# A gated scan and a top-1 mixture of experts on one core: new numbers for the planner that orders the instructions

## The chip, the core and the metric

The kernel runs on one core of a Trainium2 chip. The metric is the device time of one execution in microseconds (us). The kernel before took 938.03, 938.60 and 939.13 us in three runs; the median is 938.6 us. A profile was taken of one further execution, and all rows below come from it.

## The reference

Four sequences of 5056 steps and 256 channels run through a gated scan. The 20224 results then go, one expert each, through a two-layer network with 8 experts and 1024 hidden units.

```python
a_t     = exp(8 * sigmoid(r_gate) * log(sigmoid(a_param)))
x_gated = sqrt(max(1 - a_t * a_t, 1e-6)) * sigmoid(i_gate) * x
h       = a_t[:, t] * h + x_gated[:, t]           # over the 5056 steps
logits  = y @ w_gate + modality_bias[modality_id]
e_idx   = argmax(logits);  gate_w = softmax(logits)[e_idx]
out     = gate_w * (relu(y @ w1[e_idx]) @ w2[e_idx])
```

## The kernel before

**Chunks.** The steps are cut into 22 chunks (`STEPS`): one of 96 steps, three of 128, seventeen of 256, one of 224. A chunk's three inputs `a`, `g` and `x` (the recurrence gate, the input gate, the data) are loaded through SP's queue (L592). ScalarE (ACT) takes tanh of `g` (L636) and of `a` (L654), an exp (L660), a square and a square root (L665, L669). VectorE (DVE) takes the largest value of `x` (L840), combines the inputs (L642, L674) and runs the scan (L691). The scan's result is split into a high and a low half-precision part (ACT L888, DVE L900), which replace the input in the tile `a`.

**Routing.** TensorE (PE) computes the logits (`psl`, L913), DVE turns them into a destination index for each token (`di`, L1040), SP transposes the split result into rows (`rt<-a`, L941), and GpSimd (POOL) scatters the rows into a table in DRAM sorted by expert (`rows<-rt,di`, L1141), 128 tokens each time. Chunk 0 takes 3 such scatters, chunks 1 to 3 take 4, the chunks of 256 steps take 8. POOL also copies and adds the modality bias (`mf`, `mg`, `bm`, `bn`, L799 to L825).

**Pages.** The two experts that most tokens chose are called hot; their weights are loaded first (`wr0` to `wr3`: first and second layer of the one, then of the other), scaled and split into high and low parts (`hw0_0`, `hw0_1`, `hw1_0`, `hw1_1`; some low parts on PE and ACT as `pl`, L458, L459 and L461, others on DVE). A page is a group of rows of one expert. The first two pages of 128 rows come straight from a pick on PE (`Xfirst`). Then come twenty pages of 256 rows, from about 230 us pages of 512, and at the end four small ones. For a page SP reads the rows back transposed (`X<-rows`, L1404) with their token numbers (`mt`, L1405). PE computes the first layer into `ph` (L1502), ACT and DVE make `H` of it (L1430, L1432), PE computes the second layer into `po` (L1548), ACT scales it (`ot`, L1449), and POOL scatters it to the output (L1460). Names with a number are pages: `ph2_0` is the first quarter of the first layer of page 2, `X2` its rows. A page can't be read before the scatters that filled it have landed.

**Order.** Nothing is reordered on the chip: each engine runs its list in the order in which the program was built. A planner in Python makes that order. Each piece of work is a generator that yields an engine, an estimated duration and a condition; `run` takes the earliest startable piece, within a small window the one with the lowest rank, and emits it. The ranks are `BASE[kind] + C_STEP * chunk + RANK[kind][chunk]` (function `place`); the weights have ranks of their own (`W_RANK`, `W_LOW`). Loads have estimated landing times, which stand in `mark["load", c, name]`; work on a chunk is planned from that time. `HI` says whether ACT or DVE makes the high part of a weight, `START` the order of the first loads (a digit is a chunk, `w` a weight), `TURN` is a price on changing ACT's function table, `ON_DVE` the chunk from which small pieces move from DVE to POOL.

**Fills.** Where the plan sees PE idle for over 0.5 us (`FILL_MIN`), `fill` puts matmuls on constants there (L339, tile `fill`), 1.25 times as many as the planned gap would hold. They compute nothing that is used; they stand in PE's list like other work.

```python
n = (at - t) * FILL / 0.214 if t > COLD else (at - t) / 0.427
```

Of the kernel before, what the change touches and what calls it, by code (L numbers as in the profile page):

```python
# [18 lines left out]
B, S, D, E, FF = 4, 5056, 256, 8, 1024  # L19
# [28 lines left out]
PART = 8  # L48
BACKLOG = 6500
LOOK = 384  # L50
HI = ["A", "AD", "D", "DA", "A", "D"]
LO = "PPPDDD"
START = "0 1 w w w w 2"
MODALITY = 11.81
MODALITY_LAST = 17.39
TURN = 0.0
HALVED = 9
PACED = 2
AHEAD = 9.62
AHEAD_OF_ROWS = 2.88  # L60
LAND = 1.19
SHOW = 0.46
W_AT = 9.0
C_STEP = 3.08
GROW = 1.01
SIZE_LAG = 2.99
SIZE_LATE = 6.0
LATE = 9
LAG_LATE = 5.0
SLACK = 5.0  # L70
SLACK_EARLY = 0.0
EARLY = 7
ON_DVE = 8
BIAS_RANK = -2.93
URGENT = 0.0
ROW_STEP = 2.0
LAG = 3.0
W_RANK = [24.2, 31.2, -6.7, 1.6]
W_LOW = [6.7, 7.3, -8.0, 8.8]
PICK_AT = 8.34  # L80
PICK = 11.62


RANK = {
    "load": [0.0, 0.0, 3.0, 1.1, 0.0, 1.8, -0.6, 0.0, 0.0, 7.7],
    "scan": [0.0, 0.0, 1.5, 6.8, 1.3, -0.1, -3.1, 3.3, 0.5],
    "gate": [-2.7, -1.5, -6.0, 0.0, 0.6, -1.5, 0.0, 0.0, 0.0, -6.1],
    "size": [0.0, 0.0, 0.0, 0.0, 0.0, 0.0, 2.1, 0.0, 9.5, 4.6],
    "split": [-5.2, 0.9, 0.0, -0.5, 0.5, -2.0, 1.3, -1.3, 0.0, -1.6],
    "low": [0.0, 1.6, -3.0, -1.2, 0.0, 0.0, 5.4, 0.3, -5.6, 0.3],  # L90
    "route": [-1.2, 0.0, -3.2, -3.1, 0.0, 0.0, -4.1, 0.0, -3.7],
    "gates": [0.0, 0.0, 2.9, -2.1, 0.0, 0.0, -2.0, 0.0, -5.9],
    "rows": [-2.5, -3.4, 0.0, -9.8, 0.8, 0.0, -3.4, 2.1, -1.7],
}
BASE = {
    "load": 10, "scan": 11, "gate": 11.1, "size": 11.05, "split": 10, "low": 10, "route": 9, "gates": 9.5, "rows": 10,
# [32 lines left out]
def kernel(  # L129
# [24 lines left out]
    rows = dram.tile([NULLS + BIG, ROW], I32, name="rows")  # L154
# [24 lines left out]
    low = mb1  # L179
# [105 lines left out]
    mark = {"ch": 5.0}  # L285
# [4 lines left out]
    plan = {"end": 0.0}  # L290
# [54 lines left out]
    def run():  # L345
        while threads:
# [13 lines left out]
            turns = lambda th: eng == "ACT" and len(th.req) > 4 and th.req[4] != table[0]  # L360
            th = min(near, key=lambda th: (th.prio[eng != "PE"] + TURN * turns(th), th.start))
            dur = th.req[1]
# [69 lines left out]
    def convert(k, name, raw, to, sc, prio, urgent, then):  # L432
# [32 lines left out]
        for v in range(2):  # L465
            vs = slice(FF * v, FF * v + FF)
            src, hi = raw[:, vs], to[:, vs]
            if HI[k][v % len(HI[k])] == "A":
                yield "ACT", 1.0, None
# [8 lines left out]
    loads, seq = [], 0  # L478
    for what in START.split():
        if what == "w":  # L480
# [90 lines left out]
    def load_chunk(c):  # L571

        t0, T = CHUNKS[c]
        cols = 2 * B * T
        base = 2 * B * t0
        z = T / 256
        got = tiles[c] = []
        if f"{c}" in loads:
            yield "SP", 0.0, seen(("turn", loads.index(f"{c}") - 1)), 0.0
        else:  # L580
            yield "SP", 0.0, allof(drained(sum(B * t for _, t in CHUNKS[: c + 1]) - BACKLOG), seen(("load", c - 1))), -3.0
        n = max(1, T // P)
        for name, src in (("a", rs), ("g", gs), ("x", xs)):
            tag = "H" if c == 0 and name != "g" else name
            for i in range(n):
                yield "DMA", 2.9 * z / n, allof(room(tag) if i == 0 else seen(), paced(c)), -9.0
                if i == 0:
                    tickets[c, name] = tag, take(tag)
                    t = (pm if tag == "H" else pa).tile([P, cols], F32, name=f"{name}{c}", tag=tag, bufs=BUFS[tag])
                    got.append(t)  # L590
                w = cols // n
                ins = LOADS.dma_start(t[:, i * w : (i + 1) * w], src[:, base + i * w : base + (i + 1) * w])  # L592
                if c >= PACED:
                    tc.add_manual_dep(
                        ins.ins, pace[-2], mybir.DependencyInfo(mybir.DependencyClass.Sync, mybir.DependencyReason.DATA)
                    )
                pace.append(ins.ins.name)
                landed.append(plan["end"] + 0.1)
            mark["load", c, name] = plan["end"] + (SLACK if c >= LATE else SLACK_EARLY if c > 1 else 0.0)
        if c == 0:  # L600
            yield "DMA", 0.2, None, -9.0
            nc.sync.dma_start(wg, w_gate.rearrange("(h p) e -> p h e", p=P))
            yield "DMA", 0.2, None, -9.0
            nc.sync.dma_start(mb, mbias.rearrange("m e -> (m e)").partition_broadcast(P))
            yield "DMA", 0.5, None, -9.0
            nc.sync.dma_start(mid, modality.bitcast(I32).rearrange("p (c two) -> p c two", two=2))
        went(f"{c}")
        mark["load", c] = plan["end"]
        if c + 1 < NC:
            start_chunk(c + 1)  # L610
# [143 lines left out]
    def modality_order():  # L754
# [18 lines left out]
        while c < NC:  # L773
            n = 1
            while c + n < NC and CHUNKS[c + n][1] == CHUNKS[c][1]:
                n += 1
            add(modality_part(c, n, mq, left, tx), (0, 9 if c == 0 else min(place("load", c), MODALITY_LAST) - 0.5), plan["end"])
            c += n
# [144 lines left out]
    def rows_part(c, j):  # L923
# [759 lines left out]
```

## Time and profile before

| quantity | value |
|---|---|
| median of three runs | 938.6 us |
| the profiled execution's own time | 936.79 us |
| span of its profile | 935.1 us |
| mean granted TensorE clock | 0.996 |
| DVE, ACT, POOL busy, share of the span | 69%, 63%, 52% |
| HBM read, written | 70.86 MB, 44.48 MB |

The span runs from the first to the last instruction; 1.69 us of the execution's own time lie around it. An engine's share is its busy time over the span. Averages hide the stages here: the scan's work on DVE and ACT ends well before PE's, so a stage has to be read by a window of its own. In rows of a timeline, a bracket gives the idle time of the engine just before the row and what ended it.

### The profile page before, as it was taken

The page shows a single profiled execution, that of the slowest core. Times are in us where ns is not written, and L with a number is a line of the kernel's source. Part 1 is how long each engine was busy: PE and PEld are TensorE (multiplying, and loading weights), DVE is VectorE, ACT ScalarE, POOL GpSimd, SP SyncE. Part 2 cuts the span into 40 slices and gives each one's busy share as a digit, 9 for nine tenths or more (in the row PEclk, how much of TensorE's full clock was granted, in tenths as well). Part 3 has the DMA queues.
Part 4 walks back from the last instruction along what each step waited for, and adds up shares of the span by engine and source line. Part 5 has one row for each costly group of instructions (what it writes and reads, how often), then busy time and mean ns, then how long its engine had stood idle before and what let it go on. Part 6 is the DMA issues. An engine that isn't in the chain of part 4 may idle for free. (4 is left out here: it accounts for less than half of the span.)

```text
span 935.1 us, 19529 instructions
## 1 busy us (share of the span) xinstructions
PE 918.8 (98%) x7195; PEld 656.8 (70%) x7195; DVE 645.2 (69%) x1493; ACT 591.0 (63%) x865; POOL 487.8 (52%) x683
## 2 busy tenths in 40 slices
PE   8989899999999999999999999999999999999997
PEld 4567788888887676666666666666666666666796
DVE  7979899988788878788378767878763234423521
ACT  8978769678767777576667558577643335333422
POOL 6545467556463576466646546645664535422222
PEclk9999999999999999999999999999999999999999
DMA  8878998898969696866993985884562435213110
GB/s 312 197 211 202 244 241 247 179 284 185 229 124 225 219 197 152 254 125 160 222 214 108 251 200 159 213 229 128 117 123 72 108 104 163 80 46 125 41 43 25
DMA packets 226940, 157.90 MB, mean 169 GB/s; under 512 B 195665, under 2 KB 200146, under 8 KB 226834
## 3 DMA queue, kind: packets, MB, share of 16 engines
q1 hardware_dynamic: 210562, 112.57, 52.9%
q0 software_dynamic: 16128, 43.98, 13.7%
q8 instruction: 58, 0.95, 0.4%
q14 instruction: 48, 0.39, 0.1%
q10 hardware_dynamic: 144, 0.00, 0.0%
HBM read 70.86 MB, written 44.48 MB: 123 GB/s over the span
## 5 line engine op out<-in xcount | busy, mean ns | idle before, releaser
L1502 PE MATMUL ph<-X,hw 128*128 128x512 f16 (+1 forms) x2400 | 452.6, 333 | 6.1 <-DMA X<-rows 6.1
L1502 PEld LDWEIGHTS <-hw 128*128 128x128 f16 x2496 | 237.9, 98 | 137.3 <-DMA X<-rows 7.8
L1548 PE MATMUL po<-hw,H 128*128 128x256 f16 x2448 | 298.5, 273 | 0.1
L1460 POOL DMA_INDIRECT out_dram<-ot,mt x160 | 183.7, 1148 | 216.3 <-ACT ot L1449 167.2
L1548 PEld LDWEIGHTS <-H 128*128 128x128 f16 x2496 | 241.3, 98 | 51.1 <-issue 0.8
L1141 POOL DMA_INDIRECT rows<-rt,di x158 | 181.2, 1147 | 168.0 <-PE ph L1502 77.7
L1432 DVE SCALAR_TENSOR_TENSOR H<-ph,H 128x512 f16<-128x512 f32 (+1 forms) x216 | 143.7, 668 | 155.9 <-ACT H L1430 154.6
L1430 ACT ACTIVATE H<-ph 128x512 f16<-128x512 f32 (+1 forms) x216 | 124.0, 577 | 133.7 <-PE ph L1502 128.8
L1548 PE MATMUL po<-hw,Hb 128*128 128x256 f16 x1344 | 165.1, 273 | 0.0
L1548 PEld LDWEIGHTS <-Hb 128*128 128x128 f16 x1344 | 131.0, 98 | 36.3 <-issue 0.4
L1432 DVE SCALAR_TENSOR_TENSOR Hb<-ph,Hb 128x512 f16<-128x512 f32 x112 | 76.9, 687 | 91.4 <-ACT Hb L1430 90.7
L1449 ACT ACTIVATE ot<-po,gt 128x256 f32<-128x256 f32 x160 | 75.5, 472 | 91.4 <-PE po L1548 75.1
L1430 ACT ACTIVATE Hb<-ph 128x512 f16<-128x512 f32 x112 | 66.6, 595 | 104.7 <-PE ph L1502 102.0
L691 DVE TENSOR_TENSOR_SCAN g<-a,g 128x512 f32<-128x512 f32 (+2 forms) x77 | 94.0, 1241 | 0.6
L900 DVE SCALAR_TENSOR_TENSOR a<-g,scy,a 128x512 f16<-128x512 f32 (+3 forms) x88 | 58.2, 693 | 4.5 <-ACT a L888 4.2
L888 ACT ACTIVATE a<-g,scy 128x512 f16<-128x512 f32 (+3 forms) x88 | 55.5, 669 | 1.5 <-DVE g L691 1.5
L660 ACT ACTIVATE a<-a,ch 128x1024 f32<-128x1024 f32 (+3 forms) x44 | 49.5, 1148 | 0.0
L840 DVE TENSOR_REDUCE top<-x 128x2 f32<-128x1024 f32 (+4 forms) x35 | 46.6, 1345 | 4.2 <-DMA x<-in_x_dram 4.2
L674 DVE SCALAR_TENSOR_TENSOR g<-x,g 128x1024 f32<-128x1024 f32 (+2 forms) x39 | 47.5, 1231 | 2.1 <-ACT x L669 2.1
L642 DVE SCALAR_TENSOR_TENSOR g<-g,x 128x1024 f32<-128x1024 f32 (+2 forms) x39 | 47.6, 1232 | 0.0
L669 ACT ACTIVATE x<-x,quarter 128x1024 f32<-128x1024 f32 (+3 forms) x35 | 43.8, 1255 | 0.3
L654 ACT ACTIVATE a<-a 128x1024 f32<-128x1024 f32 (+3 forms) x35 | 40.6, 1162 | 3.4 <-DMA a<-in_r_gate_dram 3.1
(220 smaller groups left out, 666.4 us busy)
## 6 DMA issues: line engine op xcount, KB each, us to landing
a<-in_r_gate_dram SPq DMA_DIRECT2D x37, 512.0 KB
g<-in_i_gate_dram SPq DMA_DIRECT2D x37, 512.0 KB
x<-in_x_dram SPq DMA_DIRECT2D x37, 512.0 KB
wr<-in_moe_w_dram SPq DMA_DIRECT2D x4, 1024.0 KB
cw<-in_moe_w_dram SPq DMA_DIRECT2D x4, 1024.0 KB
out_dram<-ot,mt POOLq DMA_INDIRECT x160
rows<-rt,di POOLq DMA_INDIRECT x158
rt<-a SPq DMA_TRANSPOSE x88
```

What stands on the lines that cost most here:

```text
L642: nc.vector.scalar_tensor_tensor(out=g, in0=g, scalar=1.0, in1=x, op0=ALU.add, op1=ALU.mult)
L660: nc.scalar.activation(sl, sl, AF.Exp, scale=ch[:, h : h + 1], bias=ch[:, h : h + 1])
L691: nc.vector.tensor_tensor_scan(out=gi, data0=ai, data1=gi, initial=0.0, op0=ALU.mult, op1=ALU.add)
L888: nc.scalar.activation(ys[:, 0, :, g], yg[:, :, g, :].rearrange("p h (k b) -> p h k b", b=Q), AF.Copy, scale=sc[:, g : g + 1])
L900: nc.vector.scalar_tensor_tensor(out=ys[:, 1, :, g], in0=yg[:, :, g, :].rearrange("p h (k b) -> p h k b", b=Q), scalar=sc[:, g : g + 1], i ...
L1141: ins = nc.gpsimd.indirect_dma_start(out=rows[:, :], out_offset=bass.IndirectOffsetOnAxis(ap=idx, axis=0), in_=src, in_offset=None, bounds ...
L1430: nc.scalar.activation(hi, src, AF.Relu)
L1432: nc.vector.scalar_tensor_tensor(out=lo, in0=src, scalar=0.0, in1=hi, op0=ALU.max, op1=ALU.subtract)
L1449: nc.scalar.activation(t.ot[a // 2][:, a % 2, :], po, AF.Copy, scale=t.gt[:, a : a + 1])
L1460: ins = nc.gpsimd.indirect_dma_start(out=out[:, :], out_offset=bass.IndirectOffsetOnAxis(ap=t.mt[:, a, 0:1], axis=0), in_=t.ot[a // 2][:, ...
L1502: ins = nc.tensor.matmul(to, wv[:, s, k, f * P : (f + 1) * P], cur.X[:, 2 * x + k, :], start=(m == 0), stop=(m == len(mm) - 1))
L1548: ins = nc.tensor.matmul(po, H[:, hx, fi, a * P : (a + 1) * P], wv[:, wx, f], start=(f == 0 and m == 0), stop=(f == NF - 1 and m == 2))
```

## The change

Constants and rank tables of the planner get other numbers, and one line changes: a chunk's inputs were planned to be there at their estimated landing for chunks 2 to 8; now the `x` input of these chunks (the third to the ninth) is taken to land 1.2 us later. The table of ranks (`RANK`, some 80 numbers) is replaced as a whole; one row of it stands for all.

```diff
-HI = ["A", "AD", "D", "DA", "A", "D"]
+HI = ["AD", "AD", "D", "AD", "A", "D"]
-START = "0 1 w w w w 2"
-MODALITY = 11.81
-MODALITY_LAST = 17.39
-TURN = 0.0
+START = "0 w 1 w w w 2"
+MODALITY = 13.01
+MODALITY_LAST = 12.02
+TURN = 0.68
...
-AHEAD = 9.62
-AHEAD_OF_ROWS = 2.88
-LAND = 1.19
-SHOW = 0.46
-W_AT = 9.0
-C_STEP = 3.08
+AHEAD = 7.78
+AHEAD_OF_ROWS = 1.82
+LAND = 1.22
+SHOW = 0.58
+W_AT = 8
+C_STEP = 3.31
...
-SIZE_LAG = 2.99
+SIZE_LAG = 5.95
...
-SLACK_EARLY = 0.0
-EARLY = 7
-ON_DVE = 8
-BIAS_RANK = -2.93
+MARGIN = {(c, 'x'): 1.2 for c in range(2, 9)}
+EARLY = 9
+ON_DVE = 7
+BIAS_RANK = -1.39
...
-W_RANK = [24.2, 31.2, -6.7, 1.6]
-W_LOW = [6.7, 7.3, -8.0, 8.8]
-PICK_AT = 8.34
-PICK = 11.62
+W_RANK = [15.4, 22.1, -1.8, 3.8]
+W_LOW = [14.7, 8.3, -17.0, 8.6]
+PICK_AT = 8.49
+PICK = 12.87
...
-    "load": [0.0, 0.0, 3.0, 1.1, 0.0, 1.8, -0.6, 0.0, 0.0, 7.7],
+    "load": [0.0, -6.1, 0.0, 1.0, 2.9, -1.2, 1.6, -2.3, 0.0, 0.1],
...
-            mark["load", c, name] = plan["end"] + (SLACK if c >= LATE else SLACK_EARLY if c > 1 else 0.0)
+            mark["load", c, name] = plan["end"] + (SLACK if c >= LATE else MARGIN.get((c, name), 0.0))
```

What is computed stays the same, and so do the counts of the page matmuls: 3840 of the second layer (L1548) and, of the first (L1502), 192 with 128 columns, 1056 with 256 and 1344 with 512, in the same pages and in the same sizes. The fills change: 143 before, 139 now. Their places move too. Before, 70 stand ahead of `ph0_0`, the first page matmul, none from there to `po0_0`, 20 between `po0_0` and `ph2_0`, and 53 behind `ph2_0`. Now 69 stand ahead of `ph0_0`, 55 between `ph1_0` and `po0_0`, 5 between `po0_0` and `ph2_0`, and 10 behind `ph2_0`. All of them stand ahead of `ph16_0` in both. Of the second layer of page 1, 24 matmuls (`po1_0` in four groups of six) stood ahead of `ph2_0` before and stand behind it now.

Three places show how the lists move.

**TensorE, around the last two low parts of the first hot expert's second layer.** `pl1_2` and `pl1_3` are these low parts, `nid` a constant, `psl1` the counts of chunk 1. Before, both stand ahead of the first page:

```order
L458 MATMUL pl1_2_891<-wr1_285,dg1_786 128x512
L459 LDWEIGHTS nid_153
L459 MATMUL pl1_2_891<-hw0_1_229,nid_153 128x512
L458 MATMUL pl1_3_902<-wr1_285,dg1_786 128x512
L459 LDWEIGHTS nid_153
L459 MATMUL pl1_3_902<-hw0_1_229,nid_153 128x512
L1013 LDWEIGHTS um1_157
L1013 MATMUL psl1_806<-oh1_908,um1_157 128x32
```

Now they stand between fills, behind `ph0` and the first quarter of `ph1`:

```order
L339 LDWEIGHTS onesb_81
L339 MATMUL fill31_1088<-onesb_81 128x512
L458 MATMUL pl1_2_1092<-wr1_292,dg1_612 128x512
L459 LDWEIGHTS nid_153
L459 MATMUL pl1_2_1092<-hw0_1_229,nid_153 128x512
L458 MATMUL pl1_3_1102<-wr1_292,dg1_612 128x512
L459 LDWEIGHTS nid_153
L459 MATMUL pl1_3_1102<-hw0_1_229,nid_153 128x512
L339 LDWEIGHTS onesb_81
L339 MATMUL fill34_1126<-onesb_81 128x512
```

The two low parts moved behind the first page's first layer, and with them the earliest place at which `po0_0`, the first matmul of a second layer, can stand.

**ScalarE, around the inputs of chunk 4.** `a4` and `g4` are that chunk's gates, `a2` the split of chunk 2, `hw0_1` the second-layer weights of the first hot expert. Before:

```order
L654 ACTIVATE a4_928<-a4_928 128x2048
L1430 ACTIVATE H1_1020<-ph1_2_1089 128x256
L1430 ACTIVATE H1_1020<-ph1_3_1114 128x256
L660 ACTIVATE a4_928<-a4_928,ch_89 128x1024 x2
L888 ACTIVATE a2_404<-g2_453,scy2_867 128x8x32 x2
L1449 ACTIVATE ot1_0_1140<-po1_0_1141,gt1_1148 128x256
L888 ACTIVATE a2_404<-g2_453,scy2_867 128x8x32 x2
L636 ACTIVATE g4_1016<-g4_1016 128x2048
```

Now:

```order
L654 ACT_TABLE_LOAD
L654 ACTIVATE a4_952<-a4_952 128x2048
L665 ACTIVATE x3_827<-a3_746 128x1024
L636 ACTIVATE g4_1001<-g4_1001 128x2048
L461 ACTIVATE hw0_1_229<-pl1_2_1092 128x512
L888 ACTIVATE a2_428<-g2_457,scy2_1025 128x8x32 x4
L461 ACTIVATE hw0_1_229<-pl1_3_1102 128x512
L660 ACTIVATE a4_952<-a4_952,ch_89 128x1024 x2
L1430 ACTIVATE H1_969<-ph1_1_1203 128x256
```

Both tanh of chunk 4 now stand ahead of the last two weight parts, of the high split of chunk 2 and of three quarters of `H1`; before, the weight parts were long done there and the splits stood ahead of `g4`.

**GpSimd, around the scatters of chunk 0.** `mf` and `mq` belong to the modality bias; `rt0` and `di0` are the rows and indices of chunk 0. Before:

```order
L799 COPY mf_226<-mq_380 32x4
L949 TENSOR_SCALAR rt0_0_504<-tid_178 128x3
L799 COPY mf_226<-mq_380 32x3
L1141 DMA rows_78<-rt0_0_504,di0_682 164352x258 x2
L799 COPY mf_226<-mq_380 32x1
L1141 DMA rows_78<-rt0_0_504,di0_682 164352x258
L799 COPY mf_226<-mq_380 32x4
```

Now:

```order
L949 TENSOR_SCALAR rt0_0_468<-tid_178 128x3
L799 COPY mf_226<-mq_406 32x1
L799 COPY mf_226<-mq_406 32x4
L1141 DMA rows_78<-rt0_0_468,di0_719 164352x258
L799 COPY mf_226<-mq_406 32x2
L1141 DMA rows_78<-rt0_0_468,di0_719 164352x258
L799 COPY mf_226<-mq_406 32x2
L1141 DMA rows_78<-rt0_0_468,di0_719 164352x258
L799 COPY mf_226<-mq_406 32x4
```

A copy now stands behind each of the three scatters; before, the first two stood together. Before the scatters of chunk 1, POOL's list now has the bias of chunks 2, 3 and 4 (three operations each), where it had that of 3 and 4; and the bias of chunk 5 (three operations) stands ahead of the last of these scatters instead of behind it.

On SP, the first two transposes of `rt2` now stand ahead of `X2`, where all four stood behind it. The first loads stand as `a0 g0 x0 wr0 a1 g1 x1 wr1`, where `wr0` stood behind `x1`. On POOL the four scatters of chunk 2 now stand together, where two output scatters stood ahead of the last; its last scatter waits for `ph3_2`, where it waited for `po3_0`. Behind `ph16_0` the lists of PE hold the same work in both.

More of the change, by code (lines that the diff above doesn't have):

```diff
@@ L77 @@
 LAG = 3.0
-W_RANK = [24.2, 31.2, -6.7, 1.6]
-W_LOW = [6.7, 7.3, -8.0, 8.8]
-PICK_AT = 8.34
-PICK = 11.62
+W_RANK = [15.4, 22.1, -1.8, 3.8]
+W_LOW = [14.7, 8.3, -17.0, 8.6]
+PICK_AT = 8.49
+PICK = 12.87
 RANK = {
-    "load": [0.0, 0.0, 3.0, 1.1, 0.0, 1.8, -0.6, 0.0, 0.0, 7.7],
[L86 to L93, printed above, removed]
+    "load": [0.0, -6.1, 0.0, 1.0, 2.9, -1.2, 1.6, -2.3, 0.0, 0.1],
+    "scan": [0.0, 0.6, 8.3, 11.4, 1.4, -1.0, 0.0, 2.5, 0.5],
+    "gate": [0.9, 0.0, 0.0, -5.3, 0.0, -1.5, -1.2, -2.5, 0.0, 0.9],
+    "size": [0.0, -0.2, 3.8, 2.3, 0.0, 0.0, 2.7, 0.0, 6.0, 10.4],
+    "split": [1.8, 0.1, -0.4, -1.4, 0.0, -1.5, 0.0, 0.6],
+    "low": [0.0, 0.0, -1.9, 3.7, -4.0, 0.0, 1.1, 0.0, 0.3],
+    "route": [0.0, 0.0, 0.0, 0.0, 0.0, 0.0, 1.0],
+    "gates": [0.0, 1.7, 0.0, -0.8, 2.1, 0.0, 3.9, -2.5, -5.8, -2.9],
+    "rows": [-4.7, -3.5, 0.0, 5.3, 0.0, 2.0, -7.1, 0.3, 0.0, 0.9],
 }
```

## The prediction

> **What bounds the kernel now.** I read the page's shares first, then windows by stage, then what PE waits for, then the timelines of the stages that wait. The page and the windows (columns: PE, PEld, DVE, ACT, POOL busy, granted clock, DMA share, GB/s):
>
> ```profile
> PE 918.8 (98%) x7195; PEld 656.8 (70%) x7195; DVE 645.2 (69%) x1493; ACT 591.0 (63%) x865; POOL 487.8 (52%) x683
> ...
> 45.00:68.00 23.00, 19.88 (x200) 14.49 (x200) 16.62 (x50) 17.25 (x28) 12.62 (x28) 0.93 0.75 201
> 68.00:95.00 27.00, 26.85 (x233) 20.56 (x232) 25.20 (x86) 24.14 (x30) 13.35 (x14) 1.00 0.84 199
> 95.00:125.00 30.00, 27.57 (x251) 22.38 (x250) 24.69 (x58) 19.02 (x23) 15.23 (x16) 1.00 1.13 258
> 125.00:170.00 45.00, 45.00 (x424) 37.83 (x422) 42.86 (x89) 42.18 (x49) 31.45 (x26) 1.00 0.84 216
> 170.00:230.00 60.00, 58.98 (x554) 51.83 (x553) 52.42 (x127) 44.07 (x63) 35.56 (x36) 1.00 0.96 229
> ...
> 230.00:300.00 70.00, 70.00 (x648) 59.41 (x646) 58.95 (x122) 51.68 (x74) 35.92 (x46) 1.00 0.84 186
> ```
>
> PE looks full everywhere, but it isn't full of useful work. The fills alone, by window (PE busy, PEld busy, clock, DMA share, GB/s):
>
> ```profile
> 64.40:230.00 165.60, 12.25 (x53) 5.11 (x53) 0.99 0.93 223
> 230.00:935.10 705.10, 0.00 (x0) 0.00 (x0) 1.00 0.60 149
> ```
>
> From 230 us on PE is full without a fill, and its list behind `ph16_0` is the same in both orders. So this stage is a fixed price, and **the change is worth the shift of the start of `ph16_0`**, 229.33 us here. Ahead of it 53 fills and the waits below are slack on PE, while DVE is busy for 25.20 of 27, 42.86 of 45 and 52.42 of 60 us: the early stage is set by the chain from DVE over POOL's scatters and SP's reads to the next page. What PE waits for, and PE's timeline:
>
> ```profile
> PE ph L1502 <- DMA X<-rows: 6.1, 3, 2.7
> PE ph L1502 <- ACT hw L461: 1.1, 1, 1.1
> ...
> 44.98 3.51 PE L1502 MATMUL ph<-Xfirst,hw 128*128 128x128 f16 x60 [1.11 <-ACT hw L461]
> 48.33 0.82 PE L1548 MATMUL po<-hw,H 128*128 128x256 f16 x6
> 49.65 0.82 PE L1548 MATMUL po<-hw,H 128*128 128x256 f16 x6
> 50.31 0.83 PE L1502 MATMUL ph<-Xfirst,hw 128*128 128x128 f16 x12
> 64.40 2.68 PE L1502 MATMUL ph<-X,hw 128*128 128x256 f16 x12 [2.69 <-DMA X<-rows]
> 89.76 5.77 PE L339 MATMUL fill<-onesb 128*128 128x512 bf16 x26
> 95.41 5.41 PE L1502 MATMUL ph<-X,hw 128*128 128x256 f16 x48
> 103.25 1.48 PE L1502 MATMUL ph<-X,hw 128*128 128x256 f16 x12 [2.43 <-DMA X<-rows]
> 229.33 1.48 PE L1502 MATMUL ph<-X,hw 128*128 128x256 f16 x12 [1.02 <-DMA X<-rows]
> ```
>
> These are `ph2_0` at 64.40, `ph4_0` at 95.41, `ph5_0` at 103.25 and `ph16_0` at 229.33; the three waits in brackets make up the 6.1 us.
>
> **The change, part by part.** The page matmuls are the same, so only fills, places and waits count.
>
> *PE's list between `ph2_0` and `ph16_0`.* Fills fall from 53 to 10. The 26 in a row take 95.41 - 89.76 = 5.65 us, 0.217 each, so 43 fewer are -9.3 us. The 24 matmuls of `po1` that come in from ahead of `ph2_0` cost 0.66 us per six (49.65 to 50.31), +2.6. Net **-6.7 us**, if what used to hide behind the fills (the next page's scatters and reads) comes as much earlier.
>
> *The start of `ph2_0`.* Here the new order is worse, on two engines at once. POOL's and SP's timelines:
>
> ```profile
> 33.04 1.89 POOL L1141 DMA_INDIRECT rows<-rt,di  x1 [3.03 <-DVE a L900]
> 35.24 1.19 POOL L1141 DMA_INDIRECT rows<-rt,di  x1 [0.30 <-issue]
> 39.43 0.29 POOL L799 COPY mf<-mq 32x1 bf16<-32x1 bf16 x1 [3.00 <-DMA rows<-rt,di]
> 40.18 1.00 POOL L1141 DMA_INDIRECT rows<-rt,di  x1 [0.46 <-POOL mf L799]
> 45.40 1.18 POOL L799 COPY mf<-mq 32x4 bf16<-32x4 bf16 x7 [4.22 <-DMA rows<-rt,di]
> 53.48 0.97 POOL L1141 DMA_INDIRECT rows<-rt,di  x1 [0.30 <-issue]
> ...
> 45.37 0.36 SPq L1405 DMA_DIRECT2D mt<-rows  x1
> 47.49 0.43 SPq L592 DMA_DIRECT2D a<-in_r_gate_dram  x1
> 49.48 2.94 SPq L592 DMA_DIRECT2D g<-in_i_gate_dram  x2
> 59.70 1.49 SPq L1404 DMA_TRANSPOSE X<-rows  x1
> 62.05 2.54 SPq L941 DMA_TRANSPOSE rt<-a  x2
> ```
>
> A copy behind a scatter waits until that scatter has landed: from 35.24 to 40.18, 4.94 us from one scatter to the next. The new list has two such links where the old one has 2.20 + 4.94, so the third scatter is up to 2.7 us later (nothing, if the copy finds it landed). The read of `mt0` follows its landing (45.37, as the copy at 45.40), and the loads of `a4` and `g4` follow that on SP. What ACT makes of it:
>
> ```profile
> 46.13 0.59 ACT L461 ACTIVATE hw<-pl 128x512 f16<-128x512 f32 x1
> 52.10 1.91 ACT L654 ACTIVATE a<-a 128x2048 f32<-128x2048 f32 x1 [1.82 <-DMA a<-in_r_gate_dram]
> 56.71 0.90 ACT L888 ACTIVATE a<-g,scy 128x256 f16<-128x256 f32 x2
> 58.66 1.90 ACT L636 ACTIVATE g<-g 128x2048 f32<-128x2048 f32 x1
> ```
>
> ACT waits for `a4` already. It takes `g4` at 58.66 without a wait, so `g4` has landed by then, and not before 49.48 + 2.94 - 0.33 + 4.6 = 56.7 (its second half is issued at 52.1; `a4`'s took 52.10 - 47.49 = 4.6). With up to 2.7 us more that is 56.7 to 61.4; I take 60, near the upper end, because the copies' links are seen in rows and nothing in the list shortens them. Behind `g4`, on the same engine, now stand the two weight parts without which `po0_0` can't start: 1.9 of tanh, two evictions of some 0.5, four splits in 1.8 (0.90 per two), so `po0_0` at about 64.5 (from 61.2 with `g4` at 56.7, to 66). From `po0_0` to `ph2_0` PE's new list holds 36 small page matmuls (0.66 per twelve: 2.0), 24 of `po0` (2.6) and 5 fills (1.1), 5.7 us. That puts `ph2_0` at 70.2. The second path agrees: two `rt2` transposes (2.54) stand ahead of `X2` now and wait for the splits of `a2`, at 64; `X2` is issued at 66.5 and takes 59.70 to 64.40, 4.7, so 71. I take 70.0, **+5.6 us**. Its ends: if both loads are there when ACT comes, PE alone decides. `ph0_0` could then start without its wait, at 43.9; the list from there to `ph2_0` is 60 fills (13.0), eight groups of twelve small page matmuls (5.3), 24 of `po0` (2.6) and some 2 us of weight parts and small ones, so 66.8, +2.4. A shorter way to `ph0_0` would take from that, so the lower end is 0; the upper is +7.
>
> *`X5`.* In the old order SP reads `X4` and `X5` when the last scatter of chunk 2 has landed, and that one stands behind two output scatters; now they stand behind it. PE comes to `ph4` relatively later, so the 2.43 us should shrink; but DMA's share in this stage is 1.13, the highest of all, so I take half, **-1.2 us** (0 to -2.4). `X16`'s 1.02 us I leave: SP's chain ahead of it is the same in both lists.
>
> The 5 fills fewer in the cold start and the earlier `wr0` move nothing that isn't in the sum: ACT is busy for nearly all of the time up to `ph0_0` in both.
>
> **Sum:** 5.6 - 6.7 - 1.2 = **-2.3 us** on the profiled execution's own 936.79, so 934.5. That execution lies 1.8 below the median of 938.6, so the prediction is **936.3 us**. The sum asks DVE to do its work between `ph2_0` and `ph16_0` in about 157 us instead of 165; the 95% of the window from 125 to 170 shows that it can be that full.
>
> **A rule that speaks against it.** The row at 64.40 takes 2.68 us where the same twelve take 1.48 at 103.25: behind its wait, PE ran at half clock, and 1.2 us were lost; behind the 2.43 us at 103.25 nothing was lost. The Trainium skill, "TensorE: Matmul & The Clock Gate", section "Part 1: The HAM clock gate", says that PE's clock falls to half after an idle window of some 3.4 us and comes back after a busy one, and that this window runs free of the program. The trace agrees with the half clock, and with the chance in it: of two like waits one paid. By the rule, an estimate from that section would be up to 1.7 us for each fall. For the change it matters because fills are what kept PE busy in waits, and 43 of them go where waits may remain: two more falls at the row's 1.2 us would make the sum -2.3 + 2.4, no change.
>
> **The rivals.**
> 1. *The early stall isn't paid back: slower.* While ACT stands before `g4`, DVE's low split of `a2` stands behind the missing high split, and DVE has 25.20 of 27 us busy right after. If DVE paces the pages to `ph16_0`, fewer fills are only fewer fills: the room becomes waits for `X` and `H`. DVE's idle time in 68 to 230 is 162 - 145.2 = 16.8 us, about a tenth, and part of it is the way from PE over ACT back to DVE, which stays. If half of the 7.9 us is gained and the stall is 7: +3, 941.6. It decides from the point where `ph2_0` starts past 70 and `ph4_0` not before 95.4. For it: DVE's share in every window up to 170. Against it: the window from 125 to 170 has PE and DVE both nearly full.
> 2. *The loads are there: the gain comes whole.* `ph2_0` at 64.4 to 66.8, the list -6.7, `X5` -1.2: some -6, 932.6. For it: the planner gives `x` more time, so it may reach everything later. Against it: ACT waits for `a4` even now, and its place is earlier.
> 3. *It doesn't do what it says.* `ph16_0` follows a chain of reads and writes on SP from `X14` on that stands the same in both lists, and `X14` waits for the last scatter of chunk 6. If that keeps its time, `ph16_0` does, whatever comes ahead: 938 to 939. For it: the 1.02 us at 229.33. Against it: that scatter itself now waits for a page matmul of page 13 and so moves with PE.
> 4. *The clock takes it,* as above: 938.7.
>
> **How the numbers follow.** Chances: forecast 0.30, rival 1 0.27, rival 2 0.16, rival 3 0.20, rival 4 0.07. What a measurement here can tell from no change is about 0.2%, 1.9 us. Faster by more: forecast and rival 2, 0.46; within: rivals 3 and 4, 0.27; slower: rival 1, 0.27. The forecast's own range is -4.2 to -1.9 us, 934.4 to 936.7. The range has to hold both signs: down to all of rival 2 with half of `X5` back, 931.8, up to the stall at its upper end with little paid back, 942.4.
>
> **What would show it.** Right: a wait of ACT for `a` or `g` at L654 and L636 near 50 to 60 of some 4 to 8 us in sum; `ph2_0` at 68 to 72; `ph4_0` at 92 to 95; `ph6_0` earlier than before; no more than 10 fills behind `ph2_0`; `ph16_0` at 226 to 228. Wrong: `ph2_0` before 67 (rival 2); `ph4_0` after 95.4 and waits for `X` of more than 6.1 us in sum (rival 1); `ph16_0` at 229 with a wait for `X` of some us (rival 3); a granted clock near 0.5 in windows behind 70 (rival 4). It is all wrong if PE stands idle behind 230.

## The result, and the profile after

The changed kernel takes 945.76 us (median of five runs, 944.07 to 946.23), beside 938.03 us for the kernel before in the same session (934.71 to 939.13). The ratio is 1.007, its 95% interval 1.0052 to 1.0089: **slower by some 6.6 us**, where 936.3 us, a gain, was predicted, with a range up to 942.4. Its profiled execution took 944.72 us with a span of 942.9 (before: 936.79 and 935.1).

The page of the changed kernel and its windows by stage; columns as before (PE, PEld, DVE, ACT, POOL busy, granted clock, DMA share, GB/s):

```profile
PE 918.9 (97%) x7191; PEld 657.8 (70%) x7191; DVE 642.2 (68%) x1488; ACT 591.1 (63%) x864; POOL 488.6 (52%) x689
...
45.00:68.00 23.00, 19.80 (x114) 10.35 (x112) 15.88 (x48) 17.03 (x22) 12.85 (x24) 0.93 0.61 178
68.00:95.00 27.00, 27.00 (x268) 23.35 (x267) 24.53 (x75) 23.50 (x31) 13.57 (x16) 1.00 0.95 201
95.00:125.00 30.00, 26.31 (x245) 22.02 (x243) 24.46 (x69) 21.55 (x26) 15.06 (x14) 1.00 0.99 253
125.00:170.00 45.00, 43.19 (x400) 36.77 (x398) 40.22 (x84) 36.73 (x45) 31.20 (x27) 1.00 0.86 225
170.00:230.00 60.00, 56.13 (x529) 47.64 (x527) 47.93 (x115) 39.65 (x56) 33.16 (x39) 1.00 0.87 216
230.00:300.00 70.00, 67.76 (x642) 58.95 (x641) 55.84 (x113) 50.24 (x74) 36.26 (x49) 1.00 0.70 151
...
45.00:235.00 190.00, 177.43 (x1590) 144.61 (x1588) 156.96 (x394) 142.63 (x185) 108.51 (x123) 0.99 0.86 215
```

The busy sums of the page are nearly those of before (PE 918.8, DVE 645.2). Every stage from 95 to 300 us holds less of PE *and* of DVE: the same work, spread over more time. The window from 230 on, which was full before, now holds 2.24 us of idle PE.

The fills alone in the changed kernel:

```profile
64.40:230.00 165.60, 3.73 (x15) 1.47 (x15) 0.99 0.89 220
```

And the whole early part, the last of the windows above, in the kernel before:

```profile
45.00:235.00 190.00, 183.28 (x1708) 151.22 (x1708) 166.21 (x415) 150.92 (x197) 111.41 (x122) 0.99 0.91 222
```

The fills behind `ph2_0` did go: 10 are left (of the 15, 5 stand between `po0_0` and `ph2_0`). PE didn't come earlier by it. DVE did 9.25 us less in these 190 us (166.21 - 156.96), of which 2.64 between 125 and 170 us (42.86 - 40.22) and 4.49 between 170 and 230 (52.42 - 47.93): it fell behind by about the loss, and mostly late.

What PE waits for in the changed kernel, and the pages' starts on its timeline:

```profile
PE ph L1502 <- DMA X<-rows: 8.6, 9, 1.9
PE psl L913 <- ACT a L888: 2.4, 4, 1.9
...
62.13 0.22 PE L913 MATMUL psl<-a,wg 128*32 128x128 f16 x1 [1.91 <-ACT a L888]
71.50 1.47 PE L1502 MATMUL ph<-X,hw 128*128 128x256 f16 x12
98.18 5.42 PE L1502 MATMUL ph<-X,hw 128*128 128x256 f16 x48 [1.86 <-DMA X<-rows]
104.40 1.48 PE L1502 MATMUL ph<-X,hw 128*128 128x256 f16 x12 [0.81 <-DMA X<-rows]
236.28 1.48 PE L1502 MATMUL ph<-X,hw 128*128 128x256 f16 x12 [0.84 <-DMA X<-rows]
```

Three waits for pages have become nine. The places of the two profiles side by side (us; `lt5` is DVE's first step on the logits of chunk 5, `di` a chunk's destinations, made from them on DVE, and `X14` stands as SP issues it):

| start of | before | after | shift |
|---|---|---|---|
| `ph0_0` | 44.98 | 40.67 | -4.3 |
| `ph2_0` | 64.40 | 71.50 | +7.1 |
| `di3` | 91.79 | 97.00 | +5.2 |
| `ph4_0` | 95.41 | 98.18 | +2.8 |
| `di4` | 114.58 | 117.75 | +3.2 |
| `ph6_0` | 122.59 | 123.64 | +1.1 |
| `lt5` | 136.56 | 135.20 | -1.4 |
| `di5` | 141.77 | 147.56 | +5.8 |
| `ph8_0` | 145.86 | 147.78 | +1.9 |
| `di6` | 177.66 | 184.58 | +6.9 |
| `ph12_0` | 184.85 | 188.32 | +3.5 |
| `X14` | 203.07 | 211.45 | +8.4 |
| `ph16_0` | 229.33 | 236.28 | +7.0 |

On PE the early stall is paid back by page 6 but for 1.1 us, and six us are lost again between page 6 and page 16. DVE too wins it back: it comes to the logits of chunk 5 1.4 us *earlier* than before. Yet `di5`, made from these logits, is 5.8 us late, `di6` 6.9, and `X14`, which needs the rows of chunk 6, 8.4. The way from `lt5` to `di5` on DVE, in the changed kernel (shortened):

```profile
135.20 0.44 DVE L974 STREAM_TRANSPOSE lt<-psl 128x256 f32<-128x256 f32 x1
135.56 1.18 DVE L642 SCALAR_TENSOR_TENSOR g<-g,x 128x1024 f32<-128x1024 f32 x1
...
142.54 2.26 DVE L840 TENSOR_REDUCE top<-x 128x4 f32<-128x2048 f32 x1
...
145.05 2.27 DVE L840 TENSOR_REDUCE top<-x 128x4 f32<-128x2048 f32 x1
...
147.56 0.27 DVE L1040 TENSOR_REDUCE di<-dt 128x8 int32<-128x64 f32 x1
```

And before (shortened):

```profile
136.56 0.43 DVE L974 STREAM_TRANSPOSE lt<-psl 128x256 f32<-128x256 f32 x1
...
141.77 0.27 DVE L1040 TENSOR_REDUCE di<-dt 128x8 int32<-128x64 f32 x1
```

In the new list five pieces of work for chunks 6 and 7 stand on this way: three products like that at 135.56 (L642) and the two reductions (L840), 8.1 us in sum. In the old list none of them stands there, and the way takes 5.2 us instead of 12.4. So `di5` is late by the order of DVE's list; the early stall can have done no more to it than use up part of a lead.

The early stall itself, on POOL, ACT and DVE of the changed kernel:

```profile
33.74 1.17 POOL L1141 DMA_INDIRECT rows<-rt,di  x1 [3.19 <-issue]
38.58 0.18 POOL L799 COPY mf<-mq 32x2 bf16<-32x2 bf16 x1 [3.66 <-DMA rows<-rt,di]
39.32 1.13 POOL L1141 DMA_INDIRECT rows<-rt,di  x1 [0.56 <-POOL mf L799]
44.83 0.98 POOL L1141 DMA_INDIRECT rows<-rt,di  x1 [0.56 <-POOL mf L799]
...
52.38 1.28 ACT L654 ACT_TABLE_LOAD   x1 [2.86 <-DMA mt<-rows]
55.23 1.91 ACT L654 ACTIVATE a<-a 128x2048 f32<-128x2048 f32 x1 [1.57 <-DMA a<-in_r_gate_dram]
59.29 1.91 ACT L636 ACTIVATE g<-g 128x2048 f32<-128x2048 f32 x1 [1.20 <-DMA g<-in_i_gate_dram]
61.58 1.69 ACT L888 ACTIVATE a<-g,scy 128x256 f16<-128x256 f32 x4
...
62.11 1.68 DVE L900 SCALAR_TENSOR_TENSOR a<-g,scy,a 128x256 f16<-128x256 f32 x4 [6.53 <-ACT a L888]
```

The third scatter of chunk 0 comes 4.65 us later than before (44.83 against 40.18). The table load is the first half of `a4`'s step; its row names `mt`, but in the trace the first half of `a4` landed at 52.2, and SP, which waits for it too, goes on at 52.23. ACT waits for `a4` and `g4` for 5.6 us in sum, the splits of `a2` stand behind them, and DVE stands still for 6.53 us until they are made.

### The profile page after: what moved, and what is told of

The parts are those of the page before. It is cut to its first block, busy times and chain, and to the rows that moved or that the text cites. A ratio compares the mean times of both kernels' runs of the same rounds, so it can differ in the third digit from the quotient of the medians.

```text
span 942.9 us, 19526 instructions
## 1 busy us (share of the span) xinstructions
PE 918.9 (97%) x7191; PEld 657.8 (70%) x7191; DVE 642.2 (68%) x1488; ACT 591.1 (63%) x864; POOL 488.6 (52%) x689
## 3 DMA queue, kind: packets, MB, share of 16 engines
q0 software_dynamic: 16128, 43.98, 13.5%
## 5 line engine op out<-in xcount | busy, mean ns | idle before, releaser
L1502 PE MATMUL ph<-X,hw 128*128 128x512 f16 (+1 forms) x2400 | 452.5, 332 | 8.6 <-DMA X<-rows 8.6
L1502 PEld LDWEIGHTS <-hw 128*128 128x128 f16 x2496 | 238.4, 98 | 139.3 <-DMA X<-rows 10.9
L1548 PE MATMUL po<-hw,H 128*128 128x256 f16 x2448 | 300.2, 273 | 1.9 <-issue 1.2
L1548 PEld LDWEIGHTS <-H 128*128 128x128 f16 x2496 | 242.3, 98 | 53.4 <-issue 2.9
L1548 PE MATMUL po<-hw,Hb 128*128 128x256 f16 x1344 | 165.1, 273 | 0.0
L1548 PEld LDWEIGHTS <-Hb 128*128 128x128 f16 x1344 | 130.2, 98 | 34.9 <-issue 0.8
L840 DVE TENSOR_REDUCE top<-x 128x2 f32<-128x1024 f32 (+4 forms) x35 | 46.5, 1343 | 1.6 <-DMA x<-in_x_dram 1.6
L642 DVE SCALAR_TENSOR_TENSOR g<-g,x 128x1024 f32<-128x1024 f32 (+2 forms) x39 | 47.3, 1228 | 0.0
L636 ACT ACTIVATE g<-g 128x1024 f32<-128x1024 f32 (+3 forms) x35 | 39.8, 1161 | 4.2 <-DMA g<-in_i_gate_dram 4.2
```

The source lines that it names most:

```text
L1502: ins = nc.tensor.matmul(to, wv[:, s, k, f * P : (f + 1) * P], cur.X[:, 2 * x + k, :], start=(m == 0), stop=(m == len(mm) - 1))
L1548: ins = nc.tensor.matmul(po, H[:, hx, fi, a * P : (a + 1) * P], wv[:, wx, f], start=(f == 0 and m == 0), stop=(f == NF - 1 and m == 2))
```

## The experiments

Three theories. **T1:** the later part of the new order, between page 8 and page 16, where PE loses the time, is what costs it. **T2:** the stall ahead of `ph2_0` puts DVE back, DVE sets the pace of the pages and never gets the time back, so the loss is made early and only seen late. **T3:** a stand of 5.7 us of DVE near 198 us (last section) was an accident of one execution, and is the loss.

For most kernels below, the sequence in which the planner emitted its pieces was written down for both kernels and is replayed from a list, in place of the planner's choice:

```diff
-            first = min(threads, key=lambda th: th.start)
-            ...
+            th = min((th for th in threads if th.start < FAR / 2), key=lambda th: (wanted(th)[0], th.start))
```

`wanted` is a piece's place in the list. Such a list can be cut: one kernel's list up to a page's first matmul, then what remains of the other's, in its order; or one piece can be moved. The results, each against the kernel before on the same chip:

| run | what it is | median us | ratio (95% interval) |
|---|---|---|---|
| e1 | the changed kernel again | 944.64 | 1.0072 (1.0048 to 1.0096) |
| e2 | new up to page 8, then old | 946.16 | 1.0092 (1.0061 to 1.0123) |
| e3 | old up to page 8, then new | 939.68 | 1.0015 (0.9999 to 1.0031) |
| e4 | old up to page 12, then new | 934.86 | 0.9971 (0.9954 to 0.9988) |
| e5 | new, splits of `a2` first on ACT | 941.88 | 1.0062 (1.0031 to 1.0093) |
| e6 | new, one scatter first on POOL | 937.81 | 1.0042 (1.0021 to 1.0063) |
| e7 | new, both | 935.66 | 1.0027 (1.0004 to 1.0051) |
| e8 | new up to page 2, then old | 944.97 | 1.0122 (1.0070 to 1.0173) |
| e9 | old without fills | 937.24 | 0.9990 (0.9970 to 1.0009) |
| e10 | old, 4.65 us more on DVE | 943.67 | 1.0055 (1.0034 to 1.0075) |
| e11 | e7, and `bm2` to `bm4` later on POOL | 940.02 | 1.0029 (1.0013 to 1.0045) |
| e12 | old up to page 14, then new | 936.58 | 0.9996 (0.9982 to 1.0011) |
| e13 | new up to `ph0_0`, then old | 942.31 | 1.0046 (1.0026 to 1.0067) |
| e14 | old up to `ph0_0`, then new | 943.64 | 1.0062 (1.0037 to 1.0088) |
| e15 | old, new from page 12 to 14 only | 936.88 | 1.0001 (0.9986 to 1.0017) |
| e16 | e4 again | 935.96 | 0.9991 (0.9973 to 1.0008) |

Four chips were used, on which the kernel before took 934.31 to 938.13 us, so only ratios are compared between the groups e1 to e4, e5 to e8, e9 to e12 and e13 to e16. Executions of one kernel differ by several us (930 to 942 for the kernel before, on all four), so a single profile's times stand beside medians with that reserve.

### Early or late: the cuts

**e1**, the whole new list:

> The changed kernel once more, its instructions in the same order on every engine, for a second profile. Theory T1 (the later part of the new order, between ph8_0 and ph16_0, costs the time): 944 to 946 us, ph2_0 near 71.5, ph6_0 near 123.6, ph16_0 again near 236, and DVE's di7 again 10 or more us later than in the kernel before (202.7). Theory T3 (the 5.7 us near 198 us, in which DVE, ACT and POOL stood at once, were an accident of one execution): without them ph16_0 comes at 231 to 233 and the time of the profiled run is 940 to 942. If the stall is there again, T3 falls.

944.64 us, `ph16_0` at 235.0, `di7` 12.7 us late, and the stand near 198 us is there again (5.45 us). T3 as an accident falls.

**e2**, new up to `ph8_0`, old from there:

> The new order of all engines up to the first matmul of page 8 (ph8_0), the order of before from there. T1 (the later part costs the time): the first part alone leaves ph8_0 1 to 2 us later than before (145.86), and about that much at the end: 938 to 940 us, ratio 1.001 to 1.002. T2 (the early stall of 7 us has put DVE and the chains of rows back, and that surfaces later whatever order follows): 943 to 946 us, ratio 1.006 to 1.008, with ph16_0 at 234 or later.

Just above T2's range, and 6 us above T1's: the loss is made ahead of page 8. At the cut PE is 2.3 us late; `di5`, shortly ahead of it, is 5.1 us late (146.87). From there on every engine runs the old list, and PE slips to 4.7 us at page 10, 7.0 at page 13 and 7.1 at page 18, where it stays. The place of PE at the cut understated the debt; that of `di5` showed it. But this isn't all T2: `ph7_0` (127.14) and `lt5` (133.45) were 0.7 and 3.1 us *ahead* of the kernel before in this profile, and the five pieces between `lt5` and `di5` are in the part that e2 takes from the new list.

**e3**, the reverse:

> The order of before up to ph8_0, the new one from there. T1 (the later part costs the time): ph8_0 near 145.9 as before, ph16_0 at 232 to 235, and 942 to 944 us, ratio 1.005 to 1.007. T2 (the early stall does it): 937.5 to 939 us, ratio 0.999 to 1.001, ph16_0 near 229 to 230.

939.68 us: 1.4 us above the kernel before, at the edge of what can be told from nothing. T1 has room for 2.9 us at most, the upper end of the interval. The five pieces are not in this run: `di5` comes 4.8 us behind `lt5`.

**e4**, the same with the cut at page 12:

> The order of before up to the first matmul of page 12 (ph12_0, 184.85 us), the new one from there. T1 in the form that the loss arises between page 8 and page 12 (DVE's list there has 5 us more ahead of di5): close to before, 937.5 to 940 us. T1 in the form that it arises between page 12 and page 16 (the scatters of rows6 among the outs, and the chain of X14, X15, X16): 941 to 944 us. T2: 937.5 to 939 us.

934.86 us, faster than both kernels by its interval. That wasn't foreseen by any theory; e12, e15 and e16 return to it.

**e8**, the cut at page 2:

> The new order of all engines up to the first matmul of page 2 (ph2_0, 71.5 us), the order of before from there. T2 (the stall ahead of ph2_0 is enough): ph2_0 at 69 to 72, and 943 to 947 us as with the cut at page 8 (946.2). If it is the new order between page 2 and page 8 that costs the time: 938 to 941 us.

The old order behind `ph2_0` doesn't win the stall back: the largest loss of all. But `ph2_0` came at 76.97, not at 69 to 72. In this joint PE has 30 `po` matmuls and 7 fills in a row directly ahead of it, since the new list had not yet done `po1` and the old one wants it first. So e8 agrees with T2 in direction, and its size is partly its own. It hasn't the five pieces, and of the late start 8.5 us are left at page 6 and 8.8 at page 16.

### What makes the stall: single swaps in the changed kernel

**e5** moves ACT's instructions:

```diff
 (ACT)
-ACTIVATE a4<-a4 128x2048
-ACTIVATE x3<-a3 128x1024
-ACTIVATE g4<-g4 128x2048
 ACTIVATE hw0_1<-pl1_2 128x512
 ACTIVATE a2<-g2,scy2 128x8x32 x4
 ACTIVATE hw0_1<-pl1_3 128x512
+ACTIVATE a4<-a4 128x2048
+ACTIVATE x3<-a3 128x1024
+ACTIVATE g4<-g4 128x2048
```

> The changed kernel with one swap on ACT: the four splits of a2 and the last two evictions of hw0_1 stand ahead of a4's first step, x3 and g4's tanh, instead of behind them. In the changed kernel scy2 is there at 54.5 us but the splits run at 62.1, behind g4, whose load lands at 59.8; DVE idles 7.4 us for them. T2 (this stall of DVE, not paid back, is the loss): splits at about 55, psl2 at 57 to 58 instead of 62.7, ph2_0 at 65.5 to 67, ph16_0 at 229 to 231, 937.5 to 940 us. T1 (the later part of the new order costs it): ph2_0 earlier, but still 943 to 945 us. If the stall merely moves to a4's products and x4, 941 to 944 us.

What DVE waits for between 45 and 150 us in e5:

```profile
DVE top L1385 <- DMA x<-in_x_dram: 6.5, 1, 6.5
```

The splits ran at 57.0 instead of 61.6, and DVE then stood 6.5 us for `x4`, whose load SP issued at 59.0 (57.89 in the changed kernel; in this profile `mt0` was already 1.7 us later than there, at 49.70). The stall moved one load further, as the last sentence of the expectation has it: 941.88 us, little won.

**e6** moves one scatter on POOL:

```diff
 (POOL)
 DMA rows<-rt0,di0
-COPY mf<-mq 32x2
 DMA rows<-rt0,di0
+COPY mf<-mq 32x2
 COPY mf<-mq 32x2
 DMA rows<-rt0,di0
```

> The changed kernel with one swap on POOL: the third scatter of rows0 stands ahead of a copy of mf that waits for the second scatter's landing, as in the kernel before, so that one landing less (3.5 us in the profile) is waited out in the row of rows0. T2 with ACT's order as the stall: the scatters of rows1 begin some 3 us earlier, ACT's stall stays, 943 to 946 us, ratio 1.006 or more. If the scatters are what put the early part back: 939 to 942 us, with ph2_0 2.5 us earlier.

(The scatter that moves is the second of the three.) Ratio 1.0042, which is 2.8 us less than the changed kernel's 1.0072, and `ph2_0` 3.5 us earlier than in e1 (68.36): on e1's scale 941.4 us, the second case. The two intervals overlap, so the time alone doesn't settle it; the earlier `ph2_0` agrees. The scatters do put the early part back. SP's queue explains why a copy on POOL matters at all. The changed kernel's SP timeline:

```profile
47.97 0.36 SPq L1405 DMA_DIRECT2D mt<-rows  x1
48.56 0.33 SPq L592 DMA_DIRECT2D a<-in_r_gate_dram  x1
49.70 0.35 SPq L1405 DMA_DIRECT2D mt<-rows  x1
50.09 0.43 SPq L592 DMA_DIRECT2D a<-in_r_gate_dram  x1
52.23 3.33 SPq L592 DMA_DIRECT2D g<-in_i_gate_dram  x2
57.89 1.66 SPq L592 DMA_DIRECT2D x<-in_x_dram  x2
```

`mt0` is issued when the last scatter of chunk 0 has landed, and the loads of `a4`, `g4` and `x4` stand behind it in SP's queue: 2.6 us later than before (47.97 against 45.37). In e6 `mt0` goes out at 45.85 and `x4` at 54.28. ACT's order still holds the splits back there; the DVE row of e6:

```profile
DVE a L1445 <- ACT a L1433: 5.0, 1, 5.0
```

**e7**, both swaps:

> Both swaps. T2: the scatters of rows1 are then what X2 waits for; with them 3 us earlier ph2_0 comes at 64 to 66 us and the time is that of the first swap or 1 us less: 936.5 to 940 us. T1: 943 to 945 us.

Ratio 1.0027, so two small swaps give back some 4 of the 7 us, by the middle of the intervals (1 to 7, if both intervals are used). What remains may be the new order behind page 8, for which e3 leaves 1.0015, or the five pieces on DVE: in e7 `lt5` comes 4.8 us earlier than in the kernel before (131.81) and `di5` 2.4 us later (144.18). No run takes these pieces alone out of the new list, so what remains isn't divided. `ph2_0` came at 67.95, later than expected, and DVE still waited 4.4 us for `x4`.

**e11** adds a third swap:

```diff
 (POOL)
-TENSOR_TENSOR bm2, bn2, bm3, bn3, bm4, bn4 (9 in all)
 DMA rows<-rt1,di1 (4)
+TENSOR_TENSOR bm2, bn2, bm3, bn3, bm4, bn4 (9 in all)
```

> The changed kernel with both swaps of before and one more on POOL: the nine operations that make bm2, bm3 and bm4 (50 to 55 us in the changed kernel, up to 1.3 us each) stand behind the scatters of rows1 instead of ahead of them. X2 waits for the last of these scatters. T2: rows1's scatters at 48 to 53 us, X2 at 58 to 61 instead of 64.9, ph2_0 at 62 to 65, and 1 to 3 us less than with the two swaps (935.7 beside 934.3 of the kernel before): ratio 0.999 to 1.002. If the part between page 8 and page 12 costs what remains (by the cuts at 8 and at 12, 4 us), the ratio stays at 1.002 to 1.004.

A miss for the hope behind it: `X2` was issued at 61.57 and `ph2_0` came at 66.0, both earlier than with two swaps, and the time is no better (1.0029). `x4` still lands late, and `di3` to `di6` are 3 to 8 us behind the kernel before, in a profile whose execution (943.21 us) was 3.2 above its median. The list differs in one thing more: the next three operations of the bias, at 88 us in e7, come at 140. To bring page 2 forward won nothing here, where DVE wasn't brought forward.

### The step of the prediction, taken alone

**e9** takes the fills out of the kernel before: the 53 behind `ph2_0` and the 7 directly ahead of it. No other engine's list changes.

```diff
-fill x60   (between ph1 and ph16_0)
```

> The kernel before without the 60 fill matmuls that stand in its PE list between ph2_0 and ph16_0; nothing else is changed. The prediction's step (PE's list paces this stretch, so that fills taken out are time won): ph16_0 4 to 9 us earlier than 229.3, 929 to 934 us, ratio 0.990 to 0.996. Theory T2 (the loads, ACT and DVE pace it, and the fills stand in time that PE would have waited): the waits for X grow by what the fills gave up, ph16_0 at 228 to 231, ratio 0.999 to 1.002. If the clock falls without them, above 1.002.

PE's groups between 64 and 230 us, before:

```profile
L1502 PE MATMUL ph<-X,hw 128*128 128x256 f16 x679 | 81.3, 276 | 6.1 <-DMA X<-rows 6.1
L1548 PE MATMUL po<-hw,H 128*128 128x256 f16 x624 | 74.3, 273 | 0.0
L339 PE MATMUL fill<-onesb 128*128 128x512 bf16 x53 | 12.3, 379 | 0.0
```

and in e9 (last columns: busy us, mean ns of one, idle us ahead of them and its releaser):

```profile
L2047 PE MATMUL ph<-X,hw 128*128 128x256 f16 x672 | 84.8, 285 | 11.2 <-DMA X<-rows 11.2
L2093 PE MATMUL po<-hw,H 128*128 128x256 f16 x613 | 74.1, 274 | 1.5 <-DVE H L1977 0.8 <-issue 0.7
```

12.3 us of work are gone from PE and the time is the same (0.9970 to 1.0009). The rows show where most of them went: 5.1 us to longer waits for `X` (11.2 - 6.1), 1.5 us to waits ahead of `po`, and 3.5 us to slower page matmuls (285 ns against 276). So the fills stood where PE had to wait in any case. (The profiled execution took 939.96 us, 2.7 above its median, and has `ph16_0` at 231.2; part of the longer waits may be its own.)

**e10** makes one reduction of the kernel before three times:

```diff
-            nc.vector.tensor_reduce(out=top[:, gs], ...)
+            for _ in range(3 if c == 5 else 1):
+                nc.vector.tensor_reduce(out=top[:, gs], ...)
```

> The kernel before with one DVE reduction, top5 (2.26 us at 107 us, between ph5_0 and ph6_0), made three times: 4.5 us more of DVE's time, nothing else. T2 (DVE paces the pages behind it, and a delay of DVE is not won back): di5, di6 and di7 4 to 5 us later, ph16_0 at 232.5 to 234, ratio 1.003 to 1.005. The prediction's step (PE's list paces, DVE has room): ph16_0 within 1 us of 229.3, ratio 0.999 to 1.001.

```profile
104.43 6.91 DVE L1386 TENSOR_REDUCE top<-x 128x4 f32<-128x2048 f32 x3
```

4.65 us more than the single one of before (2.26) cost 5.2 us (3.2 to 7.0) at the end, with the fills all there to cover it. In its profile `di5` is 4.8 and `ph16_0` 6.7 us late. In the old order, from 107 us on, DVE sets the pace, as T2 has it, and a delay on it isn't won back; the prediction's step falls.

### What stayed open

**e13** and **e14** were to divide the stall at the first page:

> The new order up to the first matmul of the first page (ph0_0, 41 us), the order of before from there. If the part ahead of the first page (first loads, copies among the scatters of rows0) carries the loss: mt0 and the loads of a4, g4 and x4 on SP 2 to 3 us later than before, ph2_0 at 67 us or later, ratio 1.006 or more. If the order between the first page and page 2 carries it (ACT's order, hw0_1 and po1 late): 0.999 to 1.003.

> The order of before up to ph0_0 (45 us), the new one from there. If the part ahead of the first page carries the loss: near the cut at page 8 (1.0015), 1.000 to 1.003. If the order between the first page and page 2 does: 1.004 to 1.008.

Both came out slower, by 4.3 and 5.8 us, so neither half alone is free of it. But the joints bring stalls of their own: `ph0_0` starts at 49.29 in e13, later than in either kernel (44.98, 40.67), and in e14 PE idles 9.2 us ahead of one small matmul at 59.7 and `ph1_0` is 13.5 us late. They don't divide the loss.

**e12**, **e15** and **e16** follow e4's gain:

> The order of before up to the first matmul of page 14 (ph14_0, 212 us), the new one from there. With the cut at page 12 the ratio was 0.9971, with the cut at page 8 1.0015. If what the new order wins lies behind page 14 (the later chunks), 0.996 to 0.998 again; if it lies between page 12 and page 14, 0.999 to 1.001.

> The kernel before with the new order between the first matmul of page 12 and that of page 14 only. If what made the cut at page 12 faster (0.9971) lies there: 0.996 to 0.998. If it needs the new order of the later chunks too: 0.999 to 1.001.

> The cut at page 12 again (old, then new), for a narrower interval: 0.9960 to 0.9985 if the 0.9971 of three rounds holds, 0.999 to 1.001 if it was that chip and those rounds.

The cut at page 14 and the piece from 12 to 14 alone change nothing, and the cut at page 12 with more rounds gives 0.9991 (0.9973 to 1.0008). The two intervals for it overlap around 0.998. A version that surely beats the kernel before was not found.

## Why the prediction was wrong

- ***PE's list sets the time between `ph2_0` and `ph16_0`, -6.7 us: this step failed.*** Fills did fall to 10, and `po1` did come in. But the step took fills as time that PE would win, on the condition that what used to hide behind them "comes as much earlier", which nothing in the profile supported. e9 shows what they are worth: nothing (0.9990), since waits for `X` and slower matmuls take their place. With this term at 0 the sum would be 5.6 - 1.2 = +4.4 us, 943.0 with the same offset to the median, where 945.8 was measured. With the stall as measured, 7.1, and `X5` at 0 it would be 945.7, and that this meets the result is partly luck: by page 6 PE had only 1.1 us of the stall left, and the rest of the 7.0 at `ph16_0` was lost later.
- ***`ph2_0` later by 5.6 us: right in mechanism, and a little too small.*** It came at 71.50, inside 68 to 72. The copies between the scatters, `mt0` late on SP, ACT before `a4` and `g4`, and the splits behind them are all in the rows above; ACT's 5.6 us of waits are inside the 4 to 8 that were named. Two links were wrong. The third scatter was put at up to 2.7 us late and was 4.65 late; `mt0` came 2.6 late all the same, since that scatter's landing took less time than before (44.83 to 47.97, before 40.18 to 45.37), which is luck. And `po0_0` didn't wait for the last two weight parts: it ran at 59.41, not 64.5, before ACT made them (61.10 and 63.17). PE stood for the splits of `a2` instead, and the second path, over `X2`, was right: `X2` was issued at 66.92, with 66.5 forecast. e6 shows the link from POOL by undoing it; e5 undoes ACT's, and finds the next one, `x4`, behind it, which the prediction didn't have.
- ***`X5`, -1.2 us: the wait shrank, and it bought nothing.*** 2.43 became 0.81, but `ph4` now waits 1.86, and `ph5_0` is 1.15 us late all the same.
- ***The "5 fills fewer in the cold start"*** are one fewer ahead of `ph0_0` (69 against 70). Nothing hangs on it.
- ***Behind `ph16_0` all is a fixed price: nearly.*** The shift there is 7.0 us and the span grew by 7.8; PE idles 2.24 us between 230 and 300, where `X18` is issued 14.3 us later than before (253.62 against 239.35) and `di8` made 16.6 us later. The prediction named PE idle behind 230 as the sign that it is all wrong, and it was there.
- ***Rival 1 was the right one.*** "If DVE paces the pages to `ph16_0`, fewer fills are only fewer fills: the room becomes waits for `X` and `H`" is what e9 shows line by line, and e10 shows the pace, both in the old order. Its two conditions came true: `ph4_0` at 98.18, after 95.4, and waits for `X` of 8.6 us, over 6.1. Its heading, that the early stall isn't paid back, is not what PE's rows show: PE stood at +1.1 us by page 6 and lost the rest after it. Its price, 941.6, was too low because it let half of the 7.9 us be gained; none was. I gave it 0.27 and the forecast 0.30 with DVE's 25.20 of 27 and 42.86 of 45 us in the quoted rows. I read the 95% as a sign that DVE *can* be that full, when it also said that DVE had little room to make up a delay. What no line of the prediction looked at is DVE's own new order: the five pieces that now stand ahead of `di5`. How much of the 7 us they cost, beside the early stall, is open.
- ***The clock.*** Rival 4 is not what happened in the changed kernel: from 68 to 230 us its windows show 0.99 to 1.00. In e9, with more idle in PE's stretch, the granted clock between 64 and 229 us is 0.95 instead of 0.99, and this is part of why taking work from PE brought nothing. The Trainium skill, "TensorE: Matmul & The Clock Gate", section "Part 1: The HAM clock gate", says that PE's clock falls to half after an idle window of some 3.4 us. The fall is seen here, but behind shorter waits too: 2.69 us at 64.40 in the kernel before, and 2.25 us at 151.20 in e9, where the granted clock from 151.5 to 154.8 is 0.50.

T1 is left with what e3 shows, 1.4 us (-0.1 to 2.9). Not tried: the new list without the five pieces ahead of `di5`, and other orders of SP's queue, with `mt0` behind the loads of chunk 4.

## What to carry to other kernels

When two engines run nearly full side by side, look for the one on which a delay isn't won back: put a few us more on one of them and see whether they come out at the end (4.65 us on DVE cost 5.2 here, 12.3 us of filler on PE were worth nothing). Then follow the instruction that releases the next page (here `di`) through both profiles, and look at what stands newly ahead of it in its own engine's list: an engine can be on time in its sums and late with the one result that others wait for. And on SP a small read that waits (here `mt0`, 2.6 us later) holds up the loads that stand behind it (here by 2.6 to 2.9 us).

## What was not expected of the hardware

*Three engines stood at once.* In the changed kernel DVE waits for the logits of chunk 7 long after PE's row for them has ended:

```profile
197.59 0.62 PE L913 MATMUL psl<-a,wg 128*32 128x256 f16 x16
201.72 0.38 PE L1548 MATMUL po<-hw,H 128*128 128x256 f16 x2 [0.42 <-issue]
202.45 0.27 PE L1548 MATMUL po<-hw,H 128*128 128x256 f16 x1 [0.35 <-issue]
...
203.17 0.45 DVE L974 STREAM_TRANSPOSE lt<-psl 128x256 f32<-128x256 f32 x1 [5.67 <-remote]
```

A scatter on POOL (1.70) and an eviction on ACT (0.91) were released within 0.4 us of it. "remote" means that the trace has no instruction for what ended the wait. At the logits of chunk 7 it came back in e1 (5.45 us), e4 (3.99) and e16 (3.80), with the new list there, and in e13 (3.47) with the old one; e3 and e12 have 1.9 us of it at the logits of chunk 5. The profile of the kernel before has none. As e2, which lost the most but for e8, has none either, and e4 and e16 lost nothing with it, it isn't what costs the 7 us; what it is stays open.

*A small operation on POOL can take six times its time.* Two rows of one shape on POOL, and what DVE does then:

```profile
49.41 0.23 POOL L820 TENSOR_TENSOR bm<-mf,mb 128x32 f32<-128x32 bf16 x1
49.61 1.36 POOL L820 TENSOR_TENSOR bn<-mg,mb 128x32 f32<-128x32 bf16 x1
...
49.62 1.21 DVE L674 SCALAR_TENSOR_TENSOR g<-x,g 128x1024 f32<-128x1024 f32 x1
```

POOL's longer row ends about when DVE's two-input operation does (50.97 and 50.83). The Trainium skill, "SBUF — State Buffer", section "SBUF: two separate sides", has it that such an operation of DVE and one of POOL share a pair of ports that the first to come holds for the whole instruction. The trace agrees here that POOL was held; which of the two came first it doesn't tell, as POOL's row starts 0.01 us ahead. The nine of them took 5.9 us (49.41 to 55.30) ahead of the scatters of chunk 1, and in e11 moving them brought nothing that can be measured.
